# A conv and gated-scan kernel recast: two streams of 512 tokens become one stream of 960-token blocks with 40-tile cast loads

## The chip, the cores and the metric

One core of one Trainium2 chip. The metric is the time of one execution on the device in microseconds (us); lower is better. Engines are named as in the profile: PE is TensorE's matmul side and PEld its weight loads, DVE is VectorE, ACT is ScalarE, POOL is GpSimd, SP is SyncE, which issues most transfers here. A "turn" below is a DMA transpose of conv results; a "hole" is a stretch of over 3 us in which VectorE waits; a load "lands" when its completion is signalled. A "value" or "gate" product is the part of the projection that makes `val` or `gate`; the full products contract 128 channels and the half ones 64. "Granted clock" is the share of TensorE's full clock that the profile records.

## The reference, cut to what matters

```python
# x: (8, 4224, 192) float32; weight: (8, 7); w_in: (192, 1024); A_log: (512,); w_out: (512, 192)
w = softmax(weight, axis=-1)                       # 8 heads of 24 channels, 7 causal taps
c[b,s,h,g] = sum_k w[h,k] * x_pad[b, s+k, h, g]    # zero padding ahead of each of the 8 batches
val, gate = split(c @ w_in)                        # 512 + 512
h_t = a * h_(t-1) + val_t                          # a = exp(A_log), restarted for each batch
out = (silu(gate) * h) @ w_out
```

(The reference uses `a[0, 0]`, the whole row of a, so each channel has its own factor.) The tokens, 33,792 in all, pass through five stages: load and cast, conv, turn (channels go to the partitions), projections with scan and gate, output product.

## The kernel before

It runs two streams of tokens, 4 batches each, in 132 steps. A step does 512 tokens of each stream for one of four chunks of 128 channels. The 192 input channels are contracted as 128 ("full", all rows of the array) and 64 ("rest", half the rows, so that the two streams run side by side).

```python
def phase(s):
    v, gt = s + 1 < NSTEP, s >= 0
    if v:
        pv = [ps_v.tile([P, N], FP32, name=f"pv_{st}") for st in range(2)]
        ...
        full(pv, (s + 1) // NC, (s + 1) % NC)
    if gt:
        ...
        pgs = [ps_g.tile([P, N], FP32, name=f"pg_{st}") for st in range(2)]
        full(pgs, s // NC, NC + s % NC)
        rest(pgs, s // NC, NC + s % NC)
    if v:
        rest(pv, (s + 1) // NC, (s + 1) % NC)
    ...                                  # silu of the gate on ACT

def scan(s, sts=(0, 1)):                 # one scan for each stream and PSUM bank
    ...
    nc.vector.tensor_tensor_scan(h[:, o + lo : o + hi], av[:, c : c + 1].to_broadcast([P, hi - lo]),
        pv[st][:, lo:hi], initial=0.0 if lo in cuts else last[st, c], op0=Alu.mult, op1=Alu.add)

for s in range(NSTEP):
    ...                                  # conv of group gr + 1 is spread over group gr (12 steps)
    elif gr + 2 < NGR:                   # loads are for group gr + 2: 8 tiles raw, 24 with a cast
        if o in (0, 2):
            load_raw(nc.sync, gr + 2, o // 2)
        if o in (3, 9):
            load_cast(gr + 2, int(o > 8), QT, GT)
```

What is loaded in group `gr` is convolved in group `gr + 1`.

Of the kernel before, what the change touches and what calls it, by code (L numbers as in the profile page):

```python
# [10 lines left out]
FP32 = mybir.dt.float32  # L11
# [21 lines left out]
LW = 3  # L33
WARM = 26
# [3 lines left out]
def kernel(  # L38
# [16 lines left out]
    HALO = KW - 1  # L55
    P = 128
    NB = 4
    N = NB * P
    N2 = 2 * N
    T = B * S  # L60
    TS = T // 2
    NS = TS // N
    BPB = S // P
    NC = DI // P
# [3 lines left out]
    QT = 4  # L68
    QB = S // (QT * M)
    NQ = TS // (QT * M)  # L70
    GT = 16
    NGR = TS // (GT * M)
    HT = GT // 2
    SPG = GT * M // N * NC
    D1 = P
    D2R = D - P
    assert 2 * TS == T and NS * N == TS and BPB * P == S and NC == 4
    assert QB * QT * M == S and NGR * GT * M == TS and 2 * D2R == P and B % 2 == 0 and HALO <= HB
    FR = K - 1 + M
    R = 16  # L80
# [3 lines left out]
    o4 = of.rearrange("(n b p) d -> n p b d", b=NB, p=P)  # L84
# [4 lines left out]
    xraw_pool = ctx.enter_context(tc.tile_pool(name="xraw", bufs=8))  # L89
    xb_pool = ctx.enter_context(tc.tile_pool(name="xb", bufs=3))  # L90
    yc_pool = ctx.enter_context(tc.tile_pool(name="yc", bufs=2))
    xc_pool = ctx.enter_context(tc.tile_pool(name="xc", bufs=3))
    h_pool = ctx.enter_context(tc.tile_pool(name="hp", bufs=3))
    g_pool = ctx.enter_context(tc.tile_pool(name="gp", bufs=3))
    y_pool = ctx.enter_context(tc.tile_pool(name="yp", bufs=3))
    o_pool = ctx.enter_context(tc.tile_pool(name="op", bufs=3))
    ps_v = ctx.enter_context(tc.tile_pool(name="ps_v", bufs=2, space=bass.MemoryType.PSUM))
    ps_g = ctx.enter_context(tc.tile_pool(name="ps_g", bufs=1, space=bass.MemoryType.PSUM))
    ps_m = ctx.enter_context(tc.tile_pool(name="ps_m", bufs=1, space=bass.MemoryType.PSUM))


# [5 lines left out]

    xbs = {}
    raws = {}
    halos = {}  # L110

    def load(eng, t, g, st, a0, a1):

        row = st * TS + (g * GT + a0) * M - HB
        b0 = 0
        if g == 0 and a0 == 0:
            nc.gpsimd.memset(t[0:HB, 0, :], 0.0)
            eng.dma_start(t[HB:K, 0, :], xf[row + HB : row + K, :])
            b0 = 1
        eng.dma_start(  # L120
            t[:, b0 : a1 - a0, :],
            dataclasses.replace(
                xf, offset=xf.offset + (row + b0 * M) * D,
                ap=[[D, K], [M * D, a1 - a0 - b0], [1, D]],
            ),
        )
        for a in range(a0 + b0, a1):
            if (g * GT + a) % (QT * QB) == 0:
                halos.setdefault((g, a // QT), []).append(t[0:HB, a - a0, :])

    def zero_halos(g, q):
        for t in halos.pop((g, q), ()):
            nc.scalar.memzero(t)

    def load_cast(g, st, a0, a1):
        if g not in xbs:
            xbs[g] = xb_pool.tile([K, 2, GT, D], BF16, name="xb")
        load(nc.gpsimd, xbs[g][:, st, a0:a1, :], g, st, a0, a1)

    def load_raw(eng, g, st, q=0):  # L140
        if g not in xbs:
            xbs[g] = xb_pool.tile([K, 2, GT, D], BF16, name="xb")
        raws[g, st, q] = xraw_pool.tile([K, QT, D], FP32, name="xraw")
        load(eng, raws[g, st, q], g, st, q * QT, q * QT + QT)

    def cast_raw(eng, g, st, q=0):
        copy(eng, xbs[g][:, st, q * QT : q * QT + QT, :], raws.pop((g, st, q)))


    ws = singles.tile([R, H, KW], FP32, name="ws")  # L150
    nc.sync.dma_start(
        ws, dataclasses.replace(weight, ap=[[0, R], [KW, H], [1, KW]])
    )
    for st in range(2):
        load_raw((nc.scalar, nc.sync)[st], 0, st, 0)
    fz = singles.tile([R, H, FR], BF16, name="fz")
    nc.gpsimd.memset(fz, 0.0)
    wm = singles.tile([P, N], BF16, name="wm")
# [3 lines left out]
    al = singles.tile([P, NC], FP32, name="al")  # L162
    nc.gpsimd.dma_start(al, moe_A_log.rearrange("(c p) -> p c", p=P))


    def warm(ps, n):
        for _ in range(n):
            nc.tensor.matmul(ps, wm[:, 0:P], wm, start=True, stop=True)  # L168

    warm(ps_g.tile([P, N], FP32, name="pg_0"), WARM)  # L170

    wmax = singles.tile([R, H], FP32, name="wmax")
    wsum = singles.tile([R, H], FP32, name="wsum")
    winv = singles.tile([R, H], FP32, name="winv")
    nc.vector.tensor_reduce(wmax, ws, axis=mybir.AxisListType.X, op=Alu.max)
    nc.vector.tensor_tensor(
        ws, ws, wmax.unsqueeze(2).to_broadcast([R, H, KW]), op=Alu.subtract
    )
    nc.scalar.activation(ws, ws, Act.Exp)
    nc.vector.tensor_reduce(wsum, ws, axis=mybir.AxisListType.X, op=Alu.add)  # L180
    nc.vector.reciprocal(winv, wsum)
    fp = fz[:, :, K - 1 - (HB - HALO) : K - (HB - HALO)]
    nc.vector.tensor_tensor(
        dataclasses.replace(fp, ap=[fp.ap[0], fp.ap[1], [-1, KW]]), ws,
        winv.unsqueeze(2).to_broadcast([R, H, KW]), op=Alu.mult,
    )
    f_dram = nc.dram_tensor("taps_scratch", (R, H * FR), BF16, kind="Internal")
    fa = f_dram.ap()
    nc.sync.dma_start(fa, fz.rearrange("p h f -> p (h f)"))
    for st in range(2):  # L190
        load_raw(nc.sync, 0, st, 1)
    run = H * FR - K + 1
    tb = singles.tile([K, H, FR], BF16, name="tb")
    nc.sync.dma_start(
        tb.rearrange("p h f -> p (h f)")[:, 0:run],
        dataclasses.replace(fa, offset=K - 1, ap=[[H * FR - K // R, R], [-1, K // R], [1, run]]),
    )
    tb = tb[:, :, 0:M]
# [3 lines left out]
    w1r = singles.tile([P, D2], FP32, name="w1r")  # L202
    w2r = singles.tile([P, D2], FP32, name="w2r")
    nc.sync.dma_start(w1r, moe_w_in[0:D1, :])
    for m in range(0, D2, DI):
        for st in range(2):
            nc.sync.dma_start(  # L207
                w2r[st * D2R : st * D2R + D2R, m : m + DI], moe_w_in[D1:D, m : m + DI]
            )
    for q in (2, 3):  # L210
        for st in range(2):
            load_raw(nc.sync, 0, st, q)

    ident = singles.tile([M, M], BF16, name="ident")
    make_identity(nc, ident)


    av = singles.tile([P, NC], FP32, name="av")
    nc.scalar.activation(av, al, Act.Exp)
    nc.scalar.activation(quiet, av[:, 0:1], Act.Silu)  # L220

    ymain = {}
    ymix = {}
    xcs = {}

    def taps(pc, q, lo0, hi0):

        g, a = divmod(q * QT, GT)
        for h in range(H):
            lo, hi = max(h * G, lo0), min(h * G + G, hi0)  # L230
            if lo < hi:
                nc.tensor.matmul(  # L232
                    pc[:, :, :, lo - lo0 : hi - lo0], tb[:, h, :],
                    xbs[g][:, :, a : a + QT, lo:hi],
                    start=(lo == lo0), stop=(hi == hi0), skip_group_check=True,
                )

    def conv_main(eng, ps, q, split=False):

        for k in range(2):  # L240
            pc = ps[k] if split else ps[:, k * N : k * N + N]
            pc = pc[0:M, :].rearrange("p (s a d) -> p s a d", s=2, a=QT)
            taps(pc, q, k * D2R, k * D2R + D2R)
        y = yc_pool.tile([M, 2 * QT, P], BF16, name="ymain")
        yk = y.rearrange("p i (k d) -> p k i d", k=2)
        if split:
            for k in range(2):
                copy(
                    (nc.scalar, nc.vector)[k], yk[:, k, :, :],
                    ps[k][0:M, :].rearrange("p (i d) -> p i d", d=D2R),  # L250
                )
        else:
            copy(eng, yk, ps[0:M, :].rearrange("p (k i d) -> p k i d", k=2, d=D2R))
        ymain[q] = y

    def conv_mix(eng, ps, f):

        for qh in range(2):
            pc = ps[0:M, qh * N : qh * N + N].rearrange("p (a s d) -> p s a d", s=2, a=QT)
            taps(pc, 2 * f + qh, D1, D)  # L260
        y = yc_pool.tile([M, 2 * QT, P], BF16, name="ymix")
        copy(eng, y.rearrange("p t d -> p (t d)"), ps[0:M, :])
        ymix[f] = y

    def group(f):
        g, half = divmod(f, 2)
        if g not in xcs:
            xcs[g] = xc_pool.tile([P, 3, GT * M], BF16, name="xc")
        return xcs[g], half * HT * M

    def trans(xc, r, t0, n, y):
        nc.sync.dma_start_transpose(
            xc[:, r, t0 : t0 + n * M].rearrange("p (t m) -> p t m", m=M),
            y.rearrange("p t d -> p (t d)"),
        )

    def trans_main(q):
        xc, t0 = group(q // 2)
        t0 += (q % 2) * QT * M
        y = ymain.pop(q)  # L280
        for st in range(2):
            trans(xc, st, t0, QT, y[:, st * QT : st * QT + QT, :])
# [67 lines left out]
    def phase(s):  # L350
        v, gt = s + 1 < NSTEP, s >= 0
        if v:
            pv = [ps_v.tile([P, N], FP32, name=f"pv_{st}") for st in range(2)]
            pvs[s + 1] = pv
            if s < 0:
                warm(pv[0], 3)
# [223 lines left out]
```

## Time and profile before

| | before |
|---|---|
| time, median | 361.1 us (359.21 to 363.86; with the later executions of the same kernel 355 to 364) |
| steady step | 2.40 us of TensorE, 2.41 us of VectorE |
| first scan starts | 15.99 us |
| cast loads | 12 tiles, 7.5 us to landing |

Two engines that are both busy for 90% or more of the span leave little room: a gain must shorten both. The lines stand in the prediction below.

### The profile page before, as it was taken

How to read it: one execution, taken by the hardware profiler on the slowest of the kernel's cores; microseconds unless marked ns; L12 is line 12 of the kernel's file. 1: busy time of each engine (PE TensorE's matmuls, PEld its weight loads, DVE VectorE, ACT ScalarE, POOL GpSimd, SP SyncE). 2: the span in 40 equal slices, each digit the busy share in tenths (PEclk: the TensorE clock that was granted, in tenths of full speed). 3: DMA queues.
4: the chain of work that ended last, by engine and by line, in shares of the span. 5: the costliest groups of instructions: out<-in, count | busy, mean ns of one | idle time of the engine just before them, and what ended most of it. 6: DMA issues, size and time to landing. Idle time of an engine off the chain costs nothing.

```text
span 359.3 us, 7259 instructions
## 1 busy us (share of the span) xinstructions
PE 335.3 (93%) x2610; PEld 181.5 (51%) x2613; DVE 323.3 (90%) x307; ACT 271.3 (76%) x432; POOL 306.3 (85%) x174
## 2 busy tenths in 40 slices
PE   8867875999899999999999999999999999999993
PEld 3423442555455555555555555555555555555453
DVE  2589575599899999999999999999999999999993
ACT  4356675698688788879779788888888977786661
POOL 4399894599889998999999989989899898888891
PEclk9999999899999999999999999999999999999999
DMA  7949999695999999989899799799999998673324
GB/s 175 268 68 151 174 164 184 138 187 119 183 185 172 140 244 184 140 259 149 152 246 179 127 220 194 166 200 159 183 151 242 185 128 155 128 127 108 121 88 134
DMA packets 127669, 59.97 MB, mean 167 GB/s; under 512 B 81712, under 2 KB 127120, under 8 KB 127632
## 3 DMA queue, kind: packets, MB, share of 16 engines
q1 hardware_dynamic: 98208, 48.10, 62.0%
q0 software_dynamic: 28688, 10.87, 29.8%
q10 hardware_dynamic: 736, 0.53, 0.5%
q8 instruction: 20, 0.33, 0.4%
q14 instruction: 17, 0.14, 0.2%
HBM read 32.05 MB, written 26.01 MB: 162 GB/s over the span
## 4 chain that ended last, share of the span: by engine, by line
PE 81%; DMA 9%; ACT 4%; POOL 1%; issue 1%; SPq 1%; DVE 0%; ACTq 0%; DVEq 0%
PE pm L421 25%; PE pg L336 14%; PE pv L336 14%; PE pg L344 11%; PE pm L232 10%; PE pv L344 7%; DMA xb<-in_x_dram 4%; DMA xc<-ymain 2%; ACT sg L370 2%; DMA xraw<-in_x_dram 2%; POOL y L406 1%; SPq L207 1%; DMA taps_scratch<-fz 1%; ACT ymain L104 1%; PE pg L421 0%
## 5 line engine op out<-in xcount | busy, mean ns | idle before, releaser
L388 DVE TENSOR_TENSOR_SCAN h<-av,h,pv 128x512 bf16<-128x512 f32 (+3 forms) x256 | 294.5, 1210 | 19.6 <-issue 12.2
L406 POOL TENSOR_TENSOR y<-sg,h 128x1024 bf16<-128x1024 bf16 x130 | 273.6, 2124 | 34.3 <-ACT sg L370 29.9
L370 ACT ACTIVATE sg<-pg 128x512 bf16<-128x512 f32 x262 | 142.2, 595 | 36.2 <-PE pg L344 34.2
L421 PE MATMUL pm<-wout,y 128*128 128x192 bf16 x1024 | 97.2, 249 | 4.4 <-ACT ymain L104 3.1
L421 PEld LDWEIGHTS <-y 128*128 128x128 bf16 x1056 | 85.0, 98 | 30.6 <-issue 29.7
L336 PE MATMUL pv<-xc,w 128*128 128x512 bf16 x266 | 80.6, 382 | 2.9 <-DMA xc<-ymain 2.2
L336 PE MATMUL pg<-xc,w 128*128 128x512 bf16 x260 | 78.6, 381 | 0.6
L443 ACT COPY osb<-pm 128x768 f32<-128x768 f32 x63 | 50.4, 800 | 29.3 <-ACT sg L370 22.0
L336 PEld LDWEIGHTS <-w 128*128 128x128 bf16 x528 | 47.0, 98 | 38.7 <-issue 5.8
L232 PEld LDWEIGHTS <-tb 112*96 112x96 bf16 x440 | 32.8, 124 | 37.1 <-issue 35.2
L344 PE MATMUL pg<-xc,w 64*128 64x512 bf16 x262 | 51.4, 389 | 0.0
L232 PE MATMUL pm<-xb,tb 112*96 112x192 bf16 (+2 forms) x427 | 42.3, 238 | 9.1 <-ACT ymain L104 3.5
L344 PE MATMUL pv<-xc,w 64*128 64x512 bf16 x266 | 50.8, 379 | 0.0
L104 ACT CAST ymain<-pm 96x1024 bf16<-96x1024 f32 (+1 forms) x43 | 43.0, 999 | 9.4 <-PE pm L232 3.4
L344 PEld LDWEIGHTS <-w 64*128 64x128 bf16 x528 | 15.2, 94 | 58.0 <-issue 58.0
L388 DVE TENSOR_TENSOR_SCAN h<-av,pv 128x512 bf16<-128x512 f32 (+3 forms) x32 | 25.0, 796 | 0.8 <-PE pv L344 0.8
L120 POOL DMA_DIRECT2D xb<-in_x_dram x22 | 21.2, 962 | 0.0
L104 ACT CAST ymix<-pm 96x1024 bf16<-96x1024 f32 x20 | 20.2, 1010 | 0.0
L104 ACT CAST xb<-xraw 112x768 bf16<-112x768 f32 x19 | 15.8, 834 | 0.6 <-DMA xraw<-in_x_dram 0.6
L168 PE MATMUL pg<-wm 128*128 128x512 bf16 x26 | 8.6, 511 | 1.2 <-DVE wm L159 1.2
L106 POOL CAST xb<-xraw 112x768 bf16<-112x768 f32 x5 | 4.1, 826 | 3.7 <-DMA xraw<-in_x_dram 3.7
L168 PEld LDWEIGHTS <-wm 128*128 128x128 bf16 x33 | 3.8, 119 | 6.5 <-issue 3.8
(57 smaller groups left out, 38.3 us busy)
## 6 DMA issues: line engine op xcount, KB each, us to landing
out_dram<-osb SPq DMA_DIRECT2D x65, 384.0 KB, 3.4
xb<-in_x_dram POOLq DMA_DIRECT2D x18, 504.0 KB, 7.5
xraw<-in_x_dram SPq DMA_DIRECT2D x24, 336.0 KB, 5.8
xc<-ymain SPq DMA_TRANSPOSE x84, 3.6
xb<-in_x_dram POOLq DMA_DIRECT2D x4, 336.0 KB, 5.1
w1r<-in_moe_w_in_dram SPq DMA_DIRECT2D x1, 512.0 KB, 5.8
w2r<-in_moe_w_in_dram SPq DMA_DIRECT2D x4, 128.0 KB, 5.6
tb<-taps_scratch SPq DMA_DIRECT2D x1, 338.0 KB, 4.6
```

Of the source, the lines that this page charges most:

```text
L104: eng.copy(o, i)
L106: eng.tensor_copy(o, i)
L120: eng.dma_start(t[:, b0 : a1 - a0, :], dataclasses.replace(xf, offset=xf.offset + (row + b0 * M) * D, ap=[[D, K], [M * D, a1 - a0 - b0], [ ...
L168: nc.tensor.matmul(ps, wm[:, 0:P], wm, start=True, stop=True)
L232: nc.tensor.matmul(pc[:, :, :, lo - lo0 : hi - lo0], tb[:, h, :], xbs[g][:, :, a : a + QT, lo:hi], start=(lo == lo0), stop=(hi == hi0), sk ...
L336: nc.tensor.matmul(ps[st], w1[:, m * P : (m + 1) * P], xc[:, st, t], start=True, stop=False)
L344: nc.tensor.matmul(ps[st], w2[r, m * P : (m + 1) * P], xc[r, 2, t], start=False, stop=True)
L370: nc.scalar.activation(sg[:, st * N : st * N + N], pgs[st], Act.Silu)
L388: nc.vector.tensor_tensor_scan(h[:, o + lo : o + hi], av[:, c : c + 1].to_broadcast([P, hi - lo]), pv[st][:, lo:hi], initial=0.0 if lo in ...
L406: eng.tensor_mul(y, sg, h)
L421: nc.tensor.matmul(pk[b // 2][:, b % 2, :], ys[NC * i + c][:, t0 : t0 + P], wout[:, c, :], start=(b % 2 == 0 and c == 0), stop=(c == NC - ...
L443: nc.scalar.copy(osb.rearrange("p (k b) d -> p k (b d)", k=2), po)
```

## The change

Its intent: fewer and longer instructions. One stream of blocks of 10 tiles of 96 tokens (960 tokens, 480 in each of two PSUM banks), one scan over both banks, the half-row products of two steps done next to each other (one change of the array's mode each way for two steps), the tap matrix built on the chip instead of through a scratch in memory, one turn of 15 tiles a block, and, after the first four blocks, all tokens loaded by cast loads of four blocks (40 tiles). The core of the diff:

```diff
-        for st in sts:
-            for lo, hi in zip(ends, ends[1:]):
-                nc.vector.tensor_tensor_scan(h[:, o + lo : o + hi], ..., pv[st][:, lo:hi], ...)
+        for lo, hi in zip(ends, ends[1:]):
+            nc.vector.tensor_tensor_scan(h[:, lo:hi], ..., pv[:, BANK - w + lo : BANK - w + hi], ...)
...
+    for p in range(NSTEP // 2):          # two steps, s and s + 1, of block b = s // NC
+        scan(s)
+        val(s + 1, True, True)           # (step, full?, first into the bank?)
+        gate(s, True, True)
+        gate(s, False, False)
+        val(s + 1, False, False)
+        gate(s + 1, False, True)
+        silu(s)
+        mul(nc.gpsimd, s)
+        val(s + 2, False, True)
+        gate(s + 1, True, False)
+        val(s + 2, True, False)
+        silu(s + 1)
+        scan(s + 1)
+        mul(nc.gpsimd, s + 1)
+        if s % (NC * XG) == 2 * NC and b + 2 < NSB:
+            load_cast(b + 2, min(b + 2 + XG, NSB))      # XG = 4 blocks, one transfer
+        if u < NU - 1 and done_step(u) < s:
+            out_unit(u)                                 # 16 products, one copy on ACT, one store
+        ...
+        zero_halos(b + 2)                               # on ACT, where a batch starts
+        conv_piece(b + 2, p % 2)                        # 4 products, eviction; after piece 1: turn(b + 2)
```

(The passes 0 and 1 and the last one differ; cut. The PSUM tiles `pm`, two of two banks, now serve the gate, the output unit and the conv in turn.)

## The prediction

> **What bounds the kernel now.** I read the busy table first, then the chain of work that ended last, then the groups by line, then one steady stretch of the timeline, and last the ramp, where the kernel already meets the wait that matters for this change.
>
> ```profile
> PE 335.3 (93%) x2610; PEld 181.5 (51%) x2613; DVE 323.3 (90%) x307; ACT 271.3 (76%) x432; POOL 306.3 (85%) x174
> ...
> PE 81%; DMA 9%; ACT 4%; POOL 1%; issue 1%; SPq 1%; DVE 0%; ACTq 0%; DVEq 0%
> ...
> L388 DVE TENSOR_TENSOR_SCAN h<-av,h,pv 128x512 bf16<-128x512 f32 (+3 forms) x256 | 294.5, 1210 | 19.6 <-issue 12.2
> L406 POOL TENSOR_TENSOR y<-sg,h 128x1024 bf16<-128x1024 bf16 x130 | 273.6, 2124 | 34.3 <-ACT sg L370 29.9
> ...
> xb<-in_x_dram POOLq DMA_DIRECT2D x18, 504.0 KB, 7.5
> ...
> xc<-ymain SPq DMA_TRANSPOSE x84, 3.6
> xb<-in_x_dram POOLq DMA_DIRECT2D x4, 336.0 KB, 5.1
> ```
>
> TensorE and VectorE are both nearly full, so the 81% for PE names the chain, not a lone bound. A steady stretch shows how evenly they match:
>
> ```profile
> 199.99 1.50 PE L421 MATMUL pm<-wout,y 128*128 128x192 bf16 x16
> 201.32 0.59 PE L336 MATMUL pv<-xc,w 128*128 128x512 bf16 x2
> 201.75 0.59 PE L336 MATMUL pg<-xc,w 128*128 128x512 bf16 x2
> 202.28 0.39 PE L344 MATMUL pg<-xc,w 64*128 64x512 bf16 x2
> 202.50 0.38 PE L344 MATMUL pv<-xc,w 64*128 64x512 bf16 x2
> 202.81 0.64 PE L232 MATMUL pm<-xb,tb 112*96 112x128 bf16 x6
> 203.29 0.60 PE L336 MATMUL pv<-xc,w 128*128 128x512 bf16 x2
> ...
> 199.36 7.24 DVE L388 TENSOR_TENSOR_SCAN h<-av,h,pv 128x512 bf16<-128x512 f32 x6
> ```
>
> Start to start, TensorE takes 4.80 us for two steps (199.99 to the next output block at 204.79), 2.40 a step; VectorE takes 7.24 / 3 = 2.41 a step (two scans). 132 such steps are 317 us; start, ramp and tail make 359.
>
> Now the ramp. One load was issued from GpSimd at 28.73 us; a conv group wanted it early:
>
> ```profile
> 28.73 0.87 POOL L120 DMA_DIRECT2D xb<-in_x_dram  x1
> ...
> 34.18 0.98 PE L232 MATMUL pm<-xb,tb 112*96 112x192 bf16 x7 [1.35 <-DMA xb<-in_x_dram]
> ```
>
> TensorE takes its work in order: with the conv ahead of the next projection in its queue, nothing else ran until the load landed, and the clock granted afterwards was 0.50 (the windows 35 to 37 us). In the steady state this never happens, because loads are issued a whole group (12 steps) before use.
>
> **What the Trainium skill says.** "DMA: Bandwidth & Descriptors", section "Why a DMA increments its semaphore by 16 and not by 1": only the full count means that all data landed. So the first conv on a 40-tile load waits for all 40 tiles. The single wait above agrees. Same page, "Anatomy of one DMA": about 2.0 us + bytes / 436 GB/s. For 12 tiles (12 x 112 rows x 768 B = 1.03 MB read) that is 4.4 us; the page of this kernel says 7.5, so I use the trace. "TensorE: Matmul & The Clock Gate", section "What's actually happening": after an idle window of about 3.4 us the array runs at half clock, and needs about as long to recover; the trace agrees in kind (half clock for some 3.5 us after the wait at 33 us). "TensorEngine Tiling (Array Packing)", section "Key Properties": changing the tiling mode drains the array. Above, 202.28 - 201.75 = 0.53 where two full products alone take 0.43, and 202.81 - 202.50 = 0.31 where a pair of 64-row products takes 0.22: about 0.1 us each way.
>
> **The change part by part.**
> Scans. The widths 128, 256, 384 take 457, 725 and 989 ns: 2.08 ns an element. In a stream 512 elements take 1.207 us, so 1.065 + 0.142 fixed. A scan of 960 is estimated at 2.00 + 0.14 = 2.14 us. In all 135,168 elements a partition x 2.08 = 281 us, plus 164 pieces (144 steps and 5 batch borders inside blocks x 4) x 0.142 = 23; 304 against 319.5 before. Gain 15 us. A scan across two PSUM banks has no row in this trace; I assume the same rate.
> TensorE. Two steps of 960: 8 full products of 480 columns x 0.202 = 1.62; 8 half ones in 4 pairs = 0.81; one change of mode each way where there were two = 0.2; output 15 x 0.083 = 1.25 (1.33 us for 16 above); conv 8 products of 240 columns a block, 0.85, half of it here = 0.43. Sum 4.3, 2.15 a step. This again matches the scan; 4.80 x 960 / 1024 would have been 4.50, so TensorE gains about 14 us. Multiply on GpSimd: from 1155 (512) and 2124 (1024), 960 is about 2.0 us. It fits.
> Taps. The round trip through the scratch in memory goes (the first conv started at 10.80 us after its taps landed), replaced by some small products and two multiplies. First scan at about 14 us instead of 15.99. The ramp should be calmer, too: VectorE was busy only 16.7 of 20 us and 28.2 of 40 us in the windows 20 to 40 and 40 to 80.
> If every wait were hidden: 14 + 304 + 5 (ramp) + 6 (tail) = about 330 us.
>
> The loads. Read the loop: at step s = 8, 24, 40 ... (block b = 2, 6, 10 ...), after the multiply of step s + 1, GpSimd issues the load of blocks b + 2 to b + 5; in the same pass TensorE is handed the conv of block b + 2. The lead is nil. The load can't be issued earlier, since it stands in GpSimd's queue behind a multiply that needs the scan of s + 1. There are 8 such loads (b = 2 to 30). Their duration: 8 tiles 5.1 us, 12 tiles 7.5 gives 0.6 a tile and 24 us for 40; the load queue's 29.8% of 359.3 us over 248 tiles gives 0.43 a tile, 17 us and some 2 to start, so 19; alone on the engines it might be 14. I take 18. Count from the end of scan s + 1: multiply and issue at +2.4, landed at +20.4, conv and the next projection at half clock +3.2 (4 x 0.2 and six product times of 0.4), so scan s + 3 starts at +23.6 in place of +2.1. That is 21.5 us each, 8 x 21.5 = 172 us. TensorE's own even load leaves nothing to catch up with.
>
> The turns. A block's transpose (now one of 15 tiles) is issued after the second conv piece of block b + 2 in the second half of block b, and its first user is the value product in the middle of the second half of block b + 1. In quiet windows (300 to 325 us) 4 tiles landed in 2.3 to 2.4 us and 8 in 3.6 to 4.3: 0.33 to 0.48 a tile, so 15 tiles are an estimated 6 to 7.6 us; add 1.8 for ScalarE's evictions ahead of it: about 8.8. Between the conv and the user lie only about 5.7 us of TensorE's work. The loop closes by way of the next block's conv, which comes 2.6 us after the user: 8.8 + 2.6 = 11.4 a block in place of 8.6, 2.8 more. In one block of four the load's stop covers it. So some 25 x 2.8 = 70 us, less certain.
> Sum: 330 + 172 + 70 = 572.
>
> **The rivals.** (1) The wait is hidden and the gain stands: 330 us. For it: both engines' sums really shrink. Against it: the order in the loop; I see no queue in which the load could pass. (2) Only the loads bite, the turns land in time (a 15-tile transpose in 5 us or less, for instance because the per-tile cost falls in one long transfer): 330 + 172 = 502. (3) Loads run at the skill's rate, 3.44 MB in 9.9 us: the stop is 13.5, 8 of them 108, with no turn losses about 438. For it: during the stop the DMA engines have little else to do. Against: 12 tiles already miss that rate. (4) Cold clock at each turn wait, slower scans over two banks, or loads at 0.6 a tile: 620 and more.
>
> **Range and chances.** I place the time at 540, between the second case and the full sum, since the turn term may shrink and the loads run alone. 8 in 10: 450 to 615. Even with all in its favour (8 us a load, 8 stops of 11) it stays above 400, so slower has 0.96; the rest covers a misread order: faster 0.03, same 0.01.
>
> **What would show it.** In the changed profile: eight holes, about 34 us of work apart, in which TensorE and VectorE stand still for some 20 us, TensorE released by the cast load at the conv product; the cast load with a landing near 18 us; granted clock near a half after each hole; a chain with a third of the span in the load. Scans of 960 near 2.14 us and 304 in all. The turns: waits of 2 to 3 us at the half value product on the transpose, and its landing near 7 us. I am wrong if the loads land within a few us, if TensorE goes on past the conv, or if the first scan does not start near 14 us.

## The result, and the profile after

| | before | after |
|---|---|---|
| time, median | 360.15 us (4 runs) | 501.07 us (499.71 to 502.51, 4 runs) |
| span of the profiled run | 359.3 us | 498.1 us |
| PE, DVE, POOL busy | 335.3, 323.3, 306.3 us | 344.3, 310.0, 302.3 us |
| mean granted clock | 0.989 | 0.864 |

The ratio of the times is 1.394 (1.385 to 1.402).

The busy times hardly moved, and VectorE's fell by 13 us, near the 15 that the longer scans were meant to bring; the span grew by 139. So the time is in waits. The page's chain and groups of the changed kernel say which:

```profile
PE 50%; DMA 18%; ACT 13%; issue 10%; POOL 6%; DVE 3%; ACTq 0%; DVEq 0%; POOLq 0%
...
L392 DVE TENSOR_TENSOR_SCAN h<-av,h,pv 128x960 bf16<-128x960 f32 (+4 forms) x132 | 261.9, 2019 | 172.5 <-issue 158.2
...
L248 PE MATMUL pm<-xb,tb 112*96 112x240 bf16 (+1 forms) x280 | 43.2, 280 | 134.1 <-DMA xb<-in_x_dram 110.9
...
xb<-in_x_dram POOLq DMA_DIRECT2D x7, 1680.0 KB, 14.0
...
xc<-yc SPq DMA_TRANSPOSE x34, 3.8
```

The scan (L392) had 172.5 us of idle time ahead of it where the row before had 19.6, and the conv product (L248) waited 110.9 us for the load. In the time line around one of the holes the whole chain can be read off:

```profile
257.86 4.32 DVE L392 TENSOR_TENSOR_SCAN h<-av,h,pv 128x960 bf16<-128x960 f32 x2 [0.49 <-POOL y L410]
...
258.99 1.48 PE L417 MATMUL pm<-wout,y 128*128 128x192 bf16 x16
...
262.60 1.80 POOL L124 DMA_DIRECT2D xb<-in_x_dram  x1
...
276.77 1.04 PE L248 MATMUL pm<-xb,tb 112*96 112x240 bf16 x4 [16.30 <-DMA xb<-in_x_dram]
...
280.42 4.32 DVE L392 TENSOR_TENSOR_SCAN h<-av,h,pv 128x960 bf16<-128x960 f32 x2 [18.25 <-issue]
```

GpSimd issues the load at 262.60, after its multiply. TensorE has been standing at the conv product since about 260.5. The load lands 14 us after its issue; then come the conv and the next value products, and VectorE goes on at 280.42, after 18.25 us of nothing. The page names "issue" as the releaser of the scan, which only means that it found none; the time line shows the load. The windows of the same stretch (columns: length; PE, PEld, DVE, ACT, POOL busy; granted clock; DMA share, which can pass 1 in this view; GB/s) show the second, smaller cost:

```profile
272.00:276.00 4.00, 0.00 (x0) 0.00 (x0) 0.00 (x0) 0.00 (x0) 0.00 (x0) 0.50 1.31 157
276.00:280.00 4.00, 3.23 (x12) 1.52 (x14) 0.00 (x0) 0.95 (x1) 0.00 (x0) 0.50 0.01 1
```

No engine computes, and the products after the hole run at half clock. There are eight such holes of 16.3 to 18.4 us, 142.5 us together. Outside of them the profiled span of 498.1 us leaves 355.6. (The table below subtracts from the median time, 501.1, and so has 358.6.)

### The profile page after: what moved, and what is told of

It is laid out like the page before. It is cut to its first block, busy times and chain, and to the rows that moved or that the text cites. A ratio compares the mean times of both kernels' runs of the same rounds, so it can differ in the third digit from the quotient of the medians.

```text
span 498.1 us, 6635 instructions
## 1 busy us (share of the span) xinstructions
PE 344.3 (69%) x2555; PEld 200.5 (40%) x2555; DVE 310.0 (62%) x181; ACT 262.8 (53%) x372; POOL 302.3 (61%) x175
## 4 chain that ended last, share of the span: by engine, by line
PE 50%; DMA 18%; ACT 13%; issue 10%; POOL 6%; DVE 3%; ACTq 0%; DVEq 0%; POOLq 0%
DMA xb<-in_x_dram 17%; PE pm L417 15%; PE pm L352 12%; ACT osb L430 8%; PE pv L352 7%; PE pm L358 6%; POOL y L410 6%; PE pv L358 5%; DVE h L392 2%; ACT yc L101 2%; PE pm L248 2%; ACT sg L378 2%; PE pm L187 1%; DMA xc<-yc 1%; ACT xb L130 0%
## 5 line engine op out<-in xcount | busy, mean ns | idle before, releaser
L410 POOL TENSOR_TENSOR y<-sg,h 128x960 bf16<-128x960 bf16 (+2 forms) x143 | 278.4, 1967 | 184.6 <-ACT sg L378 184.0
L392 DVE TENSOR_TENSOR_SCAN h<-av,h,pv 128x960 bf16<-128x960 f32 (+4 forms) x132 | 261.9, 2019 | 172.5 <-issue 158.2
L378 ACT ACTIVATE sg<-pm 128x960 bf16<-128x960 f32 (+2 forms) x144 | 137.2, 953 | 43.4 <-PE pm L358 19.6
L248 PE MATMUL pm<-xb,tb 112*96 112x240 bf16 (+1 forms) x280 | 43.2, 280 | 134.1 <-DMA xb<-in_x_dram 110.9
L101 ACT CAST yc<-pm 96x320 bf16<-96x320 f32 (+2 forms) x140 | 69.9, 557 | 117.8 <-PE pm L248 117.6
L352 PE MATMUL pm<-xc,w 128*128 128x480 bf16 (+2 forms) x288 | 85.8, 381 | 6.3 <-ACT osb L430 0.7
L248 PEld LDWEIGHTS <-tb 112*96 112x96 bf16 x288 | 31.9, 130 | 138.5 <-DMA xb<-in_x_dram 112.5
L352 PE MATMUL pv<-xc,w 128*128 128x480 bf16 (+2 forms) x288 | 85.3, 378 | 1.7 <-DVE h L392 1.5
L358 PE MATMUL pv<-xc,w 64*128 64x480 bf16 (+2 forms) x288 | 55.4, 378 | 3.3 <-DVE h L392 2.8
L358 PE MATMUL pm<-xc,w 64*128 64x480 bf16 (+2 forms) x288 | 56.4, 386 | 0.7 <-ACT osb L430 0.7
L392 DVE TENSOR_TENSOR_SCAN h<-av,pv 128x768 bf16<-128x768 f32 (+4 forms) x32 | 45.4, 1432 | 2.6 <-PE pv L358 1.0
```

What stands on the lines that cost most here:

```text
L101: eng.copy(o, i)
L248: nc.tensor.matmul(pc[:, :, i * G : i * G + G], tb[:, h, 0:M], xt[:, a0 : a0 + n, h * G : h * G + G], start=True, stop=True, skip_group_ch ...
L352: nc.tensor.matmul(o, w1[:, m], xc[:, k * w : k * w + w], start=start, stop=not start, skip_group_check=True,)
L358: nc.tensor.matmul(o, w2[r, m], xc[r, 2 * w : 3 * w], start=start, stop=not start, skip_group_check=True,)
L378: nc.scalar.activation(sg[:, 0 : 2 * w], pgs.pop(s)[:, BANK - w : BANK + w], Act.Silu)
L392: nc.vector.tensor_tensor_scan(h[:, lo:hi], av[:, c : c + 1].to_broadcast([P, hi - lo]), pv[:, BANK - w + lo : BANK - w + hi], initial=0.0 ...
```

## The experiments

Twelve kernels ran, all correct. The rounds ran on three chips; the median of the kernel before was 359.3 to 361.3 us in each of them. "Holes" sums VectorE's waits of over 3 us in the profiled run.

| kernel | time, us | holes, us | time less holes |
|---|---|---|---|
| the changed kernel | 501.1 | 142.5 | 358.6 |
| four loads of 10, needed one last | 491.9 | 132.3 | 359.6 |
| 40-tile load one block earlier | 469.9 | 110.6 | 359.3 |
| four loads of 10, needed one first | 437.8 | 78.5 | 359.3 |
| 40-tile load one group earlier | 424.6 | 49.9 | 374.7 |
| the same, conv one block earlier too | 363.4 | none | 363.4 |
| a 10-tile load for each block, two blocks ahead | 361.8 | none | 361.8 |

The theory was that the zero lead of the loads alone makes the kernel slow; the rival, that something in the new shape (the loads' use of the DMA engines, the long turns) is slow wherever the load stands.

### Loads one group ahead

```diff
+    load_cast(XG, 2 * XG)                     # before the loop
-        if s % (NC * XG) == 2 * NC and b + 2 < NSB:
-            load_cast(b + 2, min(b + 2 + XG, NSB))
+        g2 = XG * (b // XG + 2)
+        if s % (NC * XG) == 2 * NC and g2 < NSB:
+            load_cast(g2, min(g2 + XG, NSB))
```

> Only the loads move: group 1 is loaded before the loop, and each later group one group (4 blocks, some 37 us) ahead of its first conv. Theory (the zero lead of the loads alone makes the kernel slow): the eight holes of about 18.0 us of VectorE (144 us in all) go; 501 - 144 = 357 us, that is about the time of the kernel before, and not the 330 of my sum, since the steps outside the holes take 4.65 to 4.72 us a pair and not 4.30. Rival (the load, now running beside the turns, makes the 15-tile transposes late, as they have only some 5.7 us of slack): waits at the half value product on the transpose, two blocks in four, 370 to 400 us.

Measured: 424.56 us, ratio to before 1.179 (1.169 to 1.189). The theory's 357 was missed by 67 us, and even the rival's 370 to 400 by 25. All waits on the load are gone, and a new one stands in their place:

```profile
231.72 1.80 POOL L124 DMA_DIRECT2D xb<-in_x_dram  x1
...
236.11 4.58 SPq L302 DMA_TRANSPOSE xc<-yc  x1
...
248.94 0.58 PE L359 MATMUL pv<-xc,w 64*128 64x480 bf16 x2 [7.78 <-DMA xc<-yc]
249.45 0.98 PE L353 MATMUL pm<-xc,w 128*128 128x480 bf16 x2
```

A load is issued, and 4.4 us later a turn. The turn's issue on SP takes 4.58 us (1.43 in a quiet stretch) and it lands 12.8 us after its start, where 3.8 is usual; the half value product waits 7.78 us for it, and the products behind it are at half clock again (0.50 from 249 to 253 us). The load itself now takes 19.0 us in the median. There are eight such waits of VectorE, 4.3 to 8.1 us each. So each of the two lands later when other transfers run beside it, and a lead by itself moves the wait from the load to the turn. What in the DMA engines makes the turn late no run shows.

### The same 40-tile load, one block earlier

```diff
-        if s % (NC * XG) == 2 * NC and b + 2 < NSB:
-            load_cast(b + 2, min(b + 2 + XG, NSB))
+        if s % (NC * XG) == NC and b + 3 < NSB:
+            load_cast(b + 3, min(b + 3 + XG, NSB))
```

> The same 40-tile load, issued one block (two passes, 9.3 us) earlier than in the changed kernel. Theory (hole = landing time minus lead): each hole shrinks from 18.0 by about 9.3 to 8.7 us, 501 - 8 x 9.3 = 427 us. Rival (what counts is the load's use of the DMA engines or of GpSimd, wherever it stands): stays within 20 us of 501.

Measured: 469.89 us (one look), between the two. So the expected 427 was missed, and the rival's 20 us around 501 too. The holes shrank to 13.8 in the mean (110.6 / 8), not to 8.7. The page says why: with other traffic beside it, the load took 19.9 us and not 14.0. With that, 18.0 + 5.9 - 9.3 = 14.6 was to be expected, near what came. Hole = landing time less lead holds; the landing time isn't a constant.

### Four loads of 10 tiles in the same place, in order and reversed

```diff
-            load_cast(b + 2, min(b + 2 + XG, NSB))
+            for k in range(b + 2, min(b + 2 + XG, NSB)):      # control: reversed(range(...))
+                load_cast(k, k + 1)
```

> Same place, same bytes, but four loads of 10 tiles, the block that is needed first at the head. Theory (the first conv waits for the whole transfer because one transfer signals once): it now waits for 10 tiles only, about 5.5 us in place of 14.0; holes about 9.5 us, 433 us. Rival (the engines need all of the bytes or GpSimd all of its descriptors first): no change, 500 us.

> Control of the split: the same four loads in reversed order, so the needed block comes last. Theory: as slow as the 40-tile load or a little slower, since three more issues of about 0.9 us each come before it: holes 18 to 20 us, 500 to 517 us. If smaller transfers were by themselves quicker, it would come out clearly below 500.

Measured: 437.82 and 491.94 us (one look each). Same bytes, same place, and which block comes first makes 54 us. With the needed one at the head the holes are 9.8 us in the mean, as expected. With it last they are 16.5, a little less than with one transfer (17.8), not more, as I had expected; the further issues on GpSimd (0.92 us each) overlap with the transfer. So it is the wait for one completion of 40 tiles that costs, not the moving of these bytes at that place.

### Loads one group ahead and the conv three blocks ahead

```diff
-    xc_pool = ctx.enter_context(tc.tile_pool(name="xc", bufs=3))
+    xc_pool = ctx.enter_context(tc.tile_pool(name="xc", bufs=4))
...
-            conv_piece(b + 2, p % 2)
+            conv_piece(b + 3, p % 2)          # passes 2 and 3 catch up; halos likewise
```

> The early 40-tile loads (one group ahead) as in the first run, and the conv one block earlier as well (three blocks ahead of its use, one more xc buffer), so that a turn has some 15 us instead of 5.7. Theory now: in the run with early loads, 424.6 us, the time went into turns that share the DMA engines with a 40-tile load (landing 12.5 us where 3.8 is usual, waits of 8 us of TensorE, one a group). With the longer slack these eight waits (about 60 us in all) go: 360 to 370 us. Rival (DMA as such is short while a load runs, loads, turns and output together, and the wait only moves): stays above 400.

Measured: 363.44 us, ratio 1.016 (1.000 to 1.032). The turns' waits are gone (2 us are left of 49), and with them 61 us, though the 40-tile loads still take 19.9 us to land and the turns 4.9 in the median and up to 13.8:

```profile
xb<-in_x_dram POOLq DMA_DIRECT2D x7, 1680.0 KB, 19.9
...
xc<-yc SPq DMA_TRANSPOSE x34, 4.9
```

The late turns are still there; they have slack now. So the first run's remaining 61 us were the waits for late turns and what hangs on them: 49.9 in holes, the rest not separated further (the half clock after each wait lies in it).

### A 10-tile load for each block, two blocks ahead

```diff
-        if s % (NC * XG) == 2 * NC and b + 2 < NSB:
-            load_cast(b + 2, min(b + 2 + XG, NSB))
+        if s % NC == 0 and b + 4 < NSB:
+            load_cast(b + 4, b + 5)
```

> Lead given by 10-tile loads: each block is loaded by itself, two blocks before its conv, issued half a block ahead of the turn; conv where the change has it. Theory: no holes, and a load of about 7 us is nearly over when the turn is issued, so few late turns: 355 to 370 us. Rival (any cast load beside a turn delays it past its slack): a wait in nearly every block, 400 or more.

Measured: 361.78 us, ratio 1.012 (1.000 to 1.024). Small loads land in 5.6 us, and issued half a block ahead of the turn they are nearly out of its way (turn 4.1 us). No hole is left. That takes off 139 of the 141 us of difference and lands beside the kernel before, not below it (here, as in the run just above, the interval leaves open whether it is the same or slower by up to 2 or 3%).

### Why the rest is no faster than before: the pair of steps

Without holes the kernel still takes about 360 us where I had summed 330. In the run with 10-tile loads a pair of steps takes 4.65 to 4.72 us and not 4.30:

```profile
203.48 1.48 PE L417 MATMUL pm<-wout,y 128*128 128x192 bf16 x16
204.80 0.57 PE L248 MATMUL pm<-xb,tb 112*96 112x240 bf16 x4
205.22 0.57 PE L352 MATMUL pv<-xc,w 128*128 128x480 bf16 x2
205.90 0.57 PE L352 MATMUL pm<-xc,w 128*128 128x480 bf16 x2
...
205.05 0.80 ACT L430 COPY osb<-pm 128x768 f32<-128x768 f32 x1 [0.74 <-PE pm L417]
```

Two full products need 0.41 us, but from the value product (205.22) to the gate product (205.90) it is 0.68. The gate product takes the PSUM buffer of the output unit, whose copy on ACT ends at 205.85. So 0.27 us a pair is a wait for a buffer. (The page books only 0.11 us of it as idle time of TensorE, since the matmul records overlap.) Three attempts to take it away:

```diff
 # (1) conv before the output unit
-        if u < NU - 1 and done_step(u) < s:
-            out_unit(u)
             conv_piece(b + 2, p % 2)
+        if u < NU - 1 and done_step(u) < s:
+            out_unit(u)
```

> The last one with the conv piece handed to TensorE before the output unit instead of after it. Theory for the 4.65 to 4.72 us a pair of steps where I had summed 4.30: the gate product takes the PSUM buffer that the output unit used and waits for ScalarE's copy of it (0.27 us a pair, 0.33 to 0.40 of VectorE). With the order turned round the copy lies under other work: 4.40 to 4.45 a pair, some 15 us below the run before it, 340 to 355. Rival (TensorE's own work fills the 4.7): no change within 3 us.

```diff
 # (2) = (1), and the halo zeroing earlier on ACT
-            if s % NC == 0 and b + 2 < NSB:
-                zero_halos(b + 2)
+        if s % NC == 2 and b + 3 < NSB:
+            zero_halos(b + 3)
```

> The same, and the zeroing of a batch's halo done half a block earlier on ScalarE. The changed kernel shows seven waits of TensorE on that zeroing, six of about 1.1 us and one that lies in a hole. Theory: 5 to 8 us less than the run before it. Rival (they are off the bound): same within 2 us.

Measured: 365.65 us for the first, a miss: 4 us more instead of 15 less. The output unit now takes the buffer of the second gate and waits 0.30 us for ScalarE's silu of it; a pair takes 4.84. The second: 361.74 us, so the earlier zeroing gives 3.9, less than the 5 to 8 expected and more than the rival's 2.

```diff
 # (3) early halos, conv behind the output unit; the unit bank by bank with a copy of each half
-        out_mm(ps, u, range(NC))
-        nc.scalar.copy(osb..., osrc(ps))
+        for k in range(2):
+            out_mm(ps, u, range(NC), (2 * k, 2 * k + 1))
+            nc.scalar.copy(osb[:, 2 * k : 2 * k + 2, :]..., ps[:, k * BANK : k * BANK + 2 * D])
```

> 10-tile loads two blocks ahead, halo zeroing half a block early, conv again behind the output unit; the output unit is computed bank by bank and each half copied out as soon as its eight products are done. Theory: what keeps a pair of steps at 4.65 to 4.72 us is that the gate product waits for the copy of the output unit's PSUM buffer (the turned-round order only moved that wait to the output unit, 0.30 us behind the gate's eviction). The last copy is now half as long and ends some 0.3 us earlier: 4.40 to 4.45 a pair, 361.8 - 17 - 4 = 340 to 348 us. Rival (ScalarE's order of work, with one more instruction, only moves the wait again): 356 to 362.

Measured: 383.98 us, a clear miss. The gate's wait is gone (203.40 to 203.81 below is the bare 0.41), but the second half waits for the copy of the first, though it writes the other bank: the wait that the program holds is for the tile, not for the bank. There are 65 such waits, 39.7 us in all.

```profile
200.90 0.82 PE L417 MATMUL pm<-wout,y 128*128 128x192 bf16 x8
202.33 0.82 PE L417 MATMUL pm<-wout,y 128*128 128x192 bf16 x8 [0.61 <-ACT osb L431]
202.99 0.57 PE L248 MATMUL pm<-xb,tb 112*96 112x240 bf16 x4
203.40 0.57 PE L352 MATMUL pv<-xc,w 128*128 128x480 bf16 x2
203.81 0.57 PE L352 MATMUL pm<-xc,w 128*128 128x480 bf16 x2
```

This shows the buffer wait twice over, once by its absence, but is no remedy: no run shows a shorter pair. The last run moved work across the output unit instead:

```diff
 # (4) 10-tile loads, early halos; half of the second value product behind the output unit
-            val(s + 2, True, False)
+            val(s + 2, True, False, (0,))
...
             out_unit(u)
             u += 1
+        if p != 1:
+            val(s + 2, True, False, (1,))
```

> 10-tile loads two blocks ahead (361.8 us), halo zeroing half a block early (-4 in the earlier pair of runs), whole output unit and one copy of it again; one of the two full value products of the pair's second step is handed to TensorE after the output unit instead of before it. Theory: a pair's 4.65 to 4.72 us hold 0.27 us in which the gate product waits for the copy of the output unit, while the output unit has some 0.28 us to spare behind the gate's eviction; moving 0.20 us of products across the output unit takes 0.20 us a pair off, 4.45 to 4.52: 361.8 - 4 - 14 = 344 us. The pair of halves had failed because the second half waited 0.61 us for the copy of the first, which shows the wait for the buffer but is no remedy. Rival (the value product, 1.3 us later, makes the second scan late and VectorE becomes the chain): 355 us or more.

Measured: 370.12 us, ratio 1.031 (1.026 to 1.037), the rival's case, a miss. (The 358 us from which the expectation starts, 10-tile loads with early halos and nothing else moved, was never run by itself.) The moved value product comes later, so the scan that reads it starts later, here at 204.21, and ends later; the value product two steps on takes that scan's PSUM buffer and waits for it:

```profile
205.75 0.37 PE L358 MATMUL pm<-xc,w 64*128 64x480 bf16 x2
206.47 0.38 PE L358 MATMUL pv<-xc,w 64*128 64x480 bf16 x2 [0.35 <-DVE h L392]
```

A pair takes 4.97 us. With the eight PSUM banks that the program uses in two `pv` and two `pm` tiles of two banks each, each of these orders takes one buffer's wait away and meets the next. No version tried beats the kernel before.

### What two other parts of the change are worth

Both were tried on kernel (3), each against it in the same rounds.

```diff
 # half-row products of the two steps apart again
-            gate(s + 1, False, True)
             silu(s)
             mul(nc.gpsimd, s)
-            val(s + 2, False, True)
-            gate(s + 1, True, False)
-            val(s + 2, True, False)
+            gate(s + 1, True, True)
+            val(s + 2, True, True)
+            gate(s + 1, False, False)
+            val(s + 2, False, False)
```

> The last one with the row-tile products of the two steps apart again (two changes of mode a step, not one a pair each way). Theory: two more changes of about 0.1 us a pair on TensorE; if TensorE is the bound then 70 x 0.2 = 14 us more than the run before it. Rival (VectorE's scans cover it): within 3 us of it.

```diff
 # two scans, one for each bank
-        ends = sorted(set([0] + cuts + [2 * w]))
+        ends = sorted(set([0] + cuts + [w, 2 * w]))
```

> The same as the first of these, with each scan cut at the bank's border into two of 480. Theory: 0.142 us more for each of the 144 steps on VectorE, 20 us more in its busy time (about 330 in place of 310); in the total 10 to 20 more, since VectorE is idle only some 0.1 us a pair there. Rival (a scan across two banks pays something of its own, so halves are no dearer): within 4 us.

Measured: 395.02 us without the pairing, 11.0 us more than (3), so the pairing does about what it was meant to (14 estimated). With two scans 385.94, only 2.0 more; yet VectorE's busy time went from 310.1 to 340.4 us. Two scans of 480 take 2.41 us (4.82 for four), one of 960 takes 2.16 (4.32 for two). So the one scan over two banks saves 30 us of VectorE, more than the estimate of 20, and nearly none of it reaches the end, because in that kernel TensorE's waits for ScalarE's copies set the pair (39.7 us in both runs): VectorE's idle time ahead of the scans fell from 58.5 to 30.1 us as its busy time rose. The scan's groups in kernel (3), and below them with two scans:

```profile
L392 DVE TENSOR_TENSOR_SCAN h<-av,h,pv 128x960 bf16<-128x960 f32 (+4 forms) x132 | 261.7, 2019 | 53.8 <-POOL y L410 49.6
L392 DVE TENSOR_TENSOR_SCAN h<-av,pv 128x768 bf16<-128x768 f32 (+4 forms) x32 | 45.6, 1434 | 4.7 <-POOL y L410 3.0
...
L392 DVE TENSOR_TENSOR_SCAN h<-av,h,pv 128x480 bf16<-128x480 f32 (+4 forms) x276 | 311.1, 1147 | 27.9 <-PE pv L358 21.1
L392 DVE TENSOR_TENSOR_SCAN h<-av,pv 128x384 bf16<-128x384 f32 (+4 forms) x32 | 26.6, 831 | 2.2 <-PE pv L358 2.2
```

The rival's number held for another reason than the one it gave.

## Why the prediction was right or wrong

The direction, the cause and the range held: 501 in 450 to 615, slower by the loads. Its terms were less good than the result suggests: two errors upward and one downward partly cancelled, and the 540 at which the prediction placed the time was 39 too high.

- **The lead is nil: right.** Eight holes of about 18 us with TensorE at the conv product and the load as releaser, as described. (Of the signs named, the share of the load in the chain was not met: 17%, not a third.) The two orders of the split loads show that it is the completion of the whole transfer that is waited for, and the 10-tile loads two blocks ahead remove 139 us.
- **Size of a hole: 21.5 predicted, 17.8 in the mean measured.** The term that was off is the load: 18 us assumed, 14.0 measured with the engines otherwise quiet. The other terms held: from the end of scan s + 1 to the issue some 2.6 us (2.4 predicted), from the landing to the next scan 3.65 (3.2 predicted). In all 142.5 against 172. The estimate from the contended loads of the kernel before (0.43 us a tile) was right for contended loads: 19.0 and 19.9 us in the runs with a lead.
- **The turns: 70 us predicted, none measured.** The failed step is the estimate of a 15-tile turn as 6 to 7.6 us, drawn on a line through 4 and 8 tiles. It lands in 3.8. I had named this in the second rival, whose 502 is what came; but that closeness is partly luck (next point). The slack of some 5.7 us was real, as the first experiment showed: when a turn lands in 12.8 us the kernel stops.
- **The base: 330 predicted, 355.6 measured outside the holes.** The failed step is the pair of steps at 4.30 us, a sum of TensorE's work with no room for a wait. Of the 0.35 to 0.4 us missing in the pairs shown, 0.27 is the gate product waiting for the output unit's copy, seen in the time line and gone in kernel (3); 0.08 is the output unit, which in these pairs has 16 products (1.33 us) where the sum has an average of 15 (1.25). I had read "both sums shrink" without asking whether four users of two PSUM tiles can follow one another without a gap. Besides these there are TensorE's waits of 1.1 us on the halo zeroing (4 us in all, by the second attempt above) and, where there are holes, the half clock behind each; the rest was not taken apart.
- **Scans: right.** 2.16 us for 960 elements against 2.14, 307.3 us in all (261.9 + 45.4 in the groups) against 304.
- **Taps and start: right in direction.** The first scan started at 12.28 us (14 predicted, 15.99 before).
- **The clock: right after the holes, but read too kindly in the ramp.** The prediction let the trace of the kernel before agree with an idle window of some 3.4 us ahead of the half clock. Its own line shows a wait of only 1.35 us there (last section).

So: 572 in the sum, less 70 for the turns, less 30 for the loads, plus 25 for the base makes 497, the span is 498.

The first experiment's expectation failed in the other direction: after the result I had dropped the turns altogether, since they didn't wait, and they were the first thing to wait once loads ran beside them.

## What to carry to other kernels

For each transfer, write down in which pass it is issued and in which pass its first user stands in the queue of an engine that works in order; if that is the same pass, the engine pays the whole landing time, and one large transfer makes that time longer. A lead given to a load has a price where it meets another transfer with little slack: issue many small ones between the uses rather than one large one, or give the neighbour more slack (361.8 and 363.4 us here), and look at the landing time of the neighbours. And a sum of busy times is a floor, not a forecast: where several stages share a few PSUM tiles, follow each tile from its last reader to its next writer before believing the sum.

## What the Trainium skill lacked or had wrong

- "DMA: Bandwidth & Descriptors", section "Anatomy of one DMA — SWDGE (gpsimd) path": the fit gives an estimate of 9.9 us for the 3.44 MB that a 40-tile load reads; these cast loads, in rows of 768 B read as float32 and kept as 384 B of bfloat16, took 14.0 us with the compute engines stopped and 19.0 to 19.9 beside turns and stores. The page gives no time for a cast load in rows this short.
- The same page, section "Rules for kernel authors", says that a transpose next to ordinary DMAs needs nothing. That is about correctness and agrees (all runs were correct); the rule says nothing of time, and here a 15-tile turn landed in 3.8 us in a quiet stretch and 12.8 us beside a 40-tile cast load, with its issue on SP stretched from 1.43 to 4.58 us.
- No page that I found has the time of VectorE's scan: 2.16 us for 960 elements over two PSUM banks in one instruction, 2.41 us as two of 480.
- "TensorE: Matmul & The Clock Gate", section "What's actually happening", puts the half clock after at least one idle window of about 3.4 us. The waits of 16 us agree: the granted clock was 0.50 until about 280.6 us, some 3.9 us after the products began again. But shorter waits were enough, too: in the kernel before, the clock was 1.00 until 34 us and 0.50 from 35 to 37 us, and the only waits of TensorE over 0.3 us in the six us before were 0.68 and 1.35 us long; in the run with the conv three blocks ahead it was 0.50 from 35 to 37 us after one of 1.79 us.
